# Down-projections of the second MLP as seven products for eight, for 14 of 18 pairs of chunks

## The chip, the cores and the metric

The kernel runs on one core of one Trainium2 chip. The metric is the device time of one execution in microseconds (us), as the median of several runs. The core has TensorE (PE in the rows, with its weight loads as PEld), VectorE (DVE), ScalarE (ACT), GpSimd (POOL, almost unused here) and SyncE (SP), which issues nearly all transfers.

## The reference, cut to what matters

An attention without softmax gives `x` (2304 tokens, 512 features), and two MLPs follow. All is float32; the weights of the MLPs reach the kernel as float64.

```python
h = np.maximum(x @ w_in, 0.0);  x = h * h @ moe_w_out          # first MLP, d_ff 2048
a = x @ w_a;  b = x @ w_b;      out = a * b @ moe2_w_out       # second MLP, d_ff 1536
```

## The kernel before

**Numbers.** A float32 operand of a product is kept as two halves, a rounded one (`[:, 0]`) and the rest (`[:, 1]`). A product of two operands is three matmuls into one PSUM bank: both halves of the weight with the rounded half of the data, and the rounded half of the weight with the rest of the data. ACT makes the rounded half (`copy` into an `F32R` tile), DVE the rest (`sub`). Weights are converted from float64 words to float32 (`w_float`: two ACT and four DVE instructions for 512 columns), kept in DRAM (`keep`), and fetched again for each pass and split in their slot `w` (`fetch`: a transfer, an ACT cast, a DVE subtraction).

**Stages.** After the attention and the first six chunks of the first MLP comes `rest()`: the other ten chunks of the first MLP (ph 1), then the second MLP (ph 2). Both go over the tokens in three passes of 768, each two halves j of N2 = 384 columns. In ph 2 a unit is one chunk c of 128 hidden rows: `group()` computes `a` and `b` of the chunk for both halves of the tokens as seven products for eight (42 matmuls of 384 columns, PSUM banks 4 to 7), with ACT copies from bank to bank and DVE additions between them. What it leaves is `c11` (j = 0) and `c12` (j = 1), which `lower` splits into a tile of the `gh` kind for the down-projection. For each pass `x_prep` makes the seven operands `xo` of the tokens, from seven ACT casts and eleven DVE subtractions of 768 columns, all seven without a second buffer (the seventh lies in `xb`).

**Down-projections.** `out_steps` multiplies a chunk's `gh` tile of one half j with the chunk's 512 down weights: 12 matmuls into banks 0 to 3, one job. Jobs run in runs of up to six chunks for one j and then the other; at a run's end four DVE instructions add the banks to `xt` (`evac`; a pass's first run of each j is copied). A pass has 24 jobs, 288 matmuls, and 20 such evacuations. The jobs trail the units: `due` pays out 12 matmuls' worth for each half of a unit, 2.5 units behind (`LAG`).

**Tiles.** `rest()` has eight float tiles (`ttiles`) for `p5`, `c11`, `c12`, `c22`, eight split tiles (`gtiles`), eight slots `w` for the up weights (four pieces to a unit, fetched two units ahead) and five for down weights. Conversion works in the tiles `wf`, `wl`, `we`, `raw`; the float slots `wf` and `wl` are taken in turn, eight of them.

**Order.** Every instruction is first added to `Plan` with its engines, an estimated duration and its dependencies. `Plan.order` then fixes the order of each engine's queue ahead of time: at each step an engine takes, of the instructions that are ready by the estimates, the one whose latest start is earliest. On the chip each engine follows that fixed order.

Of the kernel before, what the change touches and what calls it, by code (L numbers as in the profile page):

```python
# [22 lines left out]
P = 128  # L23
# [18 lines left out]
PIECES, OUTS = 8, 5  # L42
RUN, LAG = {1: 2, 2: 3}, {1: 4, 2: 5}

# [167 lines left out]
def tile_retention_two_mlps(  # L212
# [36 lines left out]
    def dmac(bytes_):  # L249
        return {"DMA": max(620.0, bytes_ / 260.0)}  # L250

# [61 lines left out]
    raws = []  # L313
    kept = {}

# [101 lines left out]
    def fetch(name, i, n):  # L417

        h, l = ("w", i, 0), ("w", i, 1)
        f = wslot[i].bitcast(F32)  # L420
        plan.add(dmac(P * 4 * n), dma(lambda: f[:, 1, :n], lambda: kept[name]), [("kept", name)], [l])
        plan.add({"ACT": act(n)}, copy(lambda: wslot[i][:, 0, :n], lambda: f[:, 1, :n]), [l], [h])
        plan.add(
            {"DVE": dve(n), "POOL": pool(n)},
            sub(lambda: wslot[i][:, 1, :n], lambda: f[:, 1, :n], lambda: wslot[i][:, 0, :n]), [h], [l],
        )

    def keep_out(name, src):
# [3 lines left out]
    def keep_pair(ph, c, src_a, src_b):  # L432

        a, b = slice(0, 256), slice(256, 512)
        wa, ka = w_float(src_a)
        wb, kb = w_float(src_b)
        keep((ph, c, 0), wa, ka, 512)
        ss, ks, exs = float_slot()

        def op(fn, o, co, x, cx, y, cy, r, w):  # L440
            plan.add(
                {"DVE": dve(256)},
                fn(lambda: o()[:, co], lambda: x()[:, cx], lambda: y()[:, cy]), r, w, exs,
            )
# [7 lines left out]
        keep((ph, c, 3), lambda: wa()[:, b], ka, 256)  # L452

    def keep_first(c):
# [347 lines left out]
    def enter():  # L802
# [39 lines left out]
    def rest():  # L842
# [14 lines left out]
        ttiles += [(lambda i=i: tmp[i][:, :n], ("tmp", i)) for i in range(4)]  # L857
        turn = {"t": 0, "piece": 0}
        gfree = list(gtiles)
        ofree = list(range(PIECES, PIECES + OUTS))  # L860

        def take_t():
            x, k = ttiles[turn["t"] % len(ttiles)]
            turn["t"] += 1
            plan.renew(k)
            return x, k

        def take_g():
            x, k = gfree.pop(0)
            plan.renew(k)  # L870
            return x, k

        def x_prep(ph, p):
# [8 lines left out]

            def parts(o, i, j):
# [13 lines left out]

            parts(0, 0, 0)
            comb((0, 0), (0, 1), (0, 0))
            parts(1, 0, 0)  # L900
            parts(2, 1, 0)
            comb((0, 0), (1, 1), (0, 0))
            parts(3, 0, 0)
            parts(4, 1, 1)
            comb((0, 1), (1, 1), (0, 1))
            parts(5, 0, 1)
            comb((1, 0), (1, 0), (0, 0))
            parts(6, 1, 0)

# [6 lines left out]

        units = [(ph, p, c) for ph in (1, 2) for p in range(PASSES) for c in CHUNKS[ph][::3 - ph]]
        pieces = {}

        def piece(u):  # L920
            for q in range(4):
                i = turn["piece"] % PIECES
                turn["piece"] += 1
                pieces[units[u], q] = i
                fetch((units[u][0], units[u][2], q), i, 256 if q == 3 else 512)

        outs = {}
        wanted = [(ph, p, c) for ph in (1, 2) for p in range(PASSES) for c in CHUNKS[ph]]

        def out_piece():  # L930
            if wanted:
                ph, p, c = wanted.pop(0)
                i = ofree.pop(0)
                outs[ph, p, c] = [i, 2]
                fetch((ph, c, 4), i, 512)


        PRODUCTS = [
            (0, 0, 0, 1, True), (1, 1, 0, 0, True), (3, 2, 0, 2, False), (2, 0, 256, 1, False),
            (5, 2, 256, 3, False), (4, 3, 0, 2, False), (6, 1, 256, 3, False),  # L940
        ]

        def group(unit, banks, fresh):
# [11 lines left out]
            for i, q, s, b, start in PRODUCTS:  # L955
# [14 lines left out]
                elif i == 1:  # L970
                    p5, k5 = take_t()
                    plan.add(pa, copy(p5, lambda: o[0]), [ko[0]], [k5])
                elif i == 2:
                    c11, k11 = take_t()
                    if ph == 2:
# [6 lines left out]
                elif i == 4:  # L982
                    c12, k12 = take_t()
                    plan.add({"DVE": dve(n)}, add(c12, lambda: o[2], p5), [ko[2], k5], [k12])
                    if ph == 2:
                        plan.add({"DVE": dve(n)}, mul(c12, c12, c22), [k22], [k12])
                    else:
                        relu({"ACT": act(n)}, c12, k12, c12, k12)
                        square((ph, p, 1, c), c12, k12)
                elif i == 5:  # L990
                    c22, k22 = take_t()
                    plan.add({"DVE": dve(n)}, add(c22, lambda: o[3], p5), [ko[3], k5], [k22])
# [3 lines left out]
                elif ph == 2:  # L996
                    plan.add({"DVE": dve(n)}, mul(c11, lambda: o[3], c11), [ko[3]], [k11])
                    for j, (g, kg) in enumerate(((c11, k11), (c12, k12))):
                        gh, kgh = take_g()
                        plan.add({"ACT": act(n)}, copy(lambda gh=gh: gh()[:, 0], g), [kg], [kgh + (0,)])  # L1000
                        lower((ph, p, j, c), gh, kgh, g, kg)
                else:
                    c21, k21 = take_t()
                    relu(pa, c21, k21, lambda: o[3], ko[3])
# [5 lines left out]
        def square(name, r, kr):  # L1010
            gh, kgh = take_g()
            plan.add(
# [5 lines left out]
        def lower(name, gh, kgh, g, kg):  # L1018
# [3 lines left out]
            )  # L1022
            made[name] = gh, kgh

        made = {}

        def out_steps(ph, p, j, c, start, last, round_):
            gh, kgh = made.pop((ph, p, j, c))
            c0 = (2 * p + j) * n

            def evac(m):
                d = lambda: xt[:, m, c0:c0 + n]
                kd, a, ka = tokens("xt", m, c0, n), bank[m], ("bank", m)
                if ph == 2 and round_ == 0:
                    plan.add({"ACT": act(n, True), "DVE": dve(n)}, copy(d, lambda: a[:, :n]), [ka], kd)
                else:
                    plan.add({"DVE": dve(n)}, add(d, lambda: a[:, :n], d), [ka], kd)
                if ph == 2 and c == CHUNKS[2][-1]:
                    plan.add(dmac(P * 4 * n), dma(lambda: out[:, m, c0:c0 + n], d), kd)

            wi = outs[ph, p, c][0]
# [11 lines left out]
            for m in range(KT):  # L1053
                if last:
# [3 lines left out]
                    )  # L1058
                    evac(m)
                    yield 3 / 12  # L1060
# [8 lines left out]
            gfree.append((gh, kgh))  # L1069
            outs[ph, p, c][1] -= 1  # L1070
            if not outs[ph, p, c][1]:
                ofree.append(wi)
                out_piece()

        def order(ph):
            cs, at, j, size = CHUNKS[ph], [0, 0], 0, RUN[ph]
            while min(at) < len(cs):
                a, b = at[j], min(at[j] + size, len(cs))
                yield from ((j, cs[i], i == a, i == b - 1, int(a > 0)) for i in range(a, b))
                at[j], j, size = b, 1 - j, 2 * RUN[ph]  # L1080

        downs = (s for ph in (1, 2) for p in range(PASSES) for d in order(ph) for s in out_steps(ph, p, *d))
        due = -LAG[1]

        x_prep(1, 0)
        piece(0)
# [3 lines left out]
        for u, unit in enumerate(units):  # L1090
            ph, p, c = unit
            if u and units[u - 1][:2] != (ph, p):
                x_prep(ph, p)
                if (ph, p) == (2, 0):
                    due -= LAG[2] - LAG[1]
            for _ in group(unit, (4, 5, 6, 7), u == 0):
                due += {1: 4, 2: 2}[ph] / 14
                while due > 1e-6:
                    due -= next(downs)
            if u + 2 < len(units):  # L1100
# [93 lines left out]
```

## Time and profile before

| | us |
|---|---|
| median of 3 runs (862.95 to 863.95) | 863.61 |
| profiled execution, its own time | 864.91 |
| span in its trace, first to last instruction | 863.2 |
| PE busy | 847.3 |
| PEld busy | 816.7 |
| DVE busy | 665.8 |
| ACT busy | 545.8 |

The span lies 1.7 us under the profiled execution's own time. Busy times are of merged intervals: where instructions of one engine overlap, the overlap counts once. A pipelined PE is shown as busy although each matmul's shown duration is longer than the distance to the next.

### The profile page before, as it was taken

How to read it: one execution, taken by the hardware profiler on the slowest of the kernel's cores; microseconds unless marked ns; L12 is line 12 of the kernel's file. 1: busy time of each engine (PE TensorE's matmuls, PEld its weight loads, DVE VectorE, ACT ScalarE, POOL GpSimd, SP SyncE). 2: the span in 40 equal slices, each digit the busy share in tenths (PEclk: the TensorE clock that was granted, in tenths of full speed). 3: DMA queues.
4: the chain of work that ended last, by engine and by line, in shares of the span. 5: the costliest groups of instructions: out<-in, count | busy, mean ns of one | idle time of the engine just before them, and what ended most of it. 6: DMA issues, size and time to landing. Idle time of an engine off the chain costs nothing.

```text
span 863.2 us, 17321 instructions
## 1 busy us (share of the span) xinstructions
PE 847.3 (98%) x6624; PEld 816.7 (95%) x6624; DVE 665.8 (77%) x1338; ACT 545.8 (63%) x1077; POOL 0.7 (0%) x6
## 2 busy tenths in 40 slices
PE   5999999999999999999999999999999999999998
PEld 5888888889999999999999999999999999999998
DVE  5999784987699999999999987597555577655553
ACT  3676562777788787978885665475555465555530
POOL 0000000000000000000000000000000000000000
PEclk9999999999999999999999999999999999999999
DMA  8776872478776678567846876335333344443322
GB/s 298 249 265 216 282 220 60 132 234 259 268 231 194 208 236 245 173 221 249 256 135 214 247 255 213 87 104 171 112 113 110 90 119 129 135 115 93 110 56 74
DMA packets 76195, 154.89 MB, mean 179 GB/s; under 512 B 8400, under 2 KB 20816, under 8 KB 76112
## 3 DMA queue, kind: packets, MB, share of 16 engines
q1 hardware_dynamic: 75968, 153.78, 56.9%
q8 instruction: 52, 0.85, 0.4%
q14 instruction: 31, 0.25, 0.1%
q10 hardware_dynamic: 144, 0.01, 0.0%
HBM read 122.95 MB, written 30.80 MB: 178 GB/s over the span
## 4 chain that ended last, share of the span: by engine, by line
PE 95%; DVE 3%; issue 1%; ACT 0%; DMA 0%; ACTq 0%
PE bank L229 95%; DVE wf L394 1%; DVE wf L383 0%; DMA vt<-vtab 0%; DVE xt L620 0%; DVE sa L657 0%; DVE pt L635 0%; DVE xt L241 0%; DVE wf L375 0%; DVE wf L368 0%; DVE w L238 0%; ACT we L390 0%; ACT tv L548 0%; DVE gh L238 0%; DVE xb L238 0%
## 5 line engine op out<-in xcount | busy, mean ns | idle before, releaser
L229 PE MATMUL bank<-xo,w 128*128 128x384 f32 x1838 | 410.4, 334 | 0.0
L229 PEld LDWEIGHTS bank<-xo,w 128*128 128x128 f32 x1838 | 326.7, 188 | 0.0
L229 PE MATMUL bank<-xb,w 128*128 128x384 f32 (+2 forms) x1050 | 239.7, 347 | 0.9 <-ACT r L759 0.7
L235 ACT CAST w<-w 128x512 fp32r<-128x512 f32 (+1 forms) x270 | 153.4, 579 | 90.0 <-DMA w<-kept 80.4
L229 PEld LDWEIGHTS bank<-xb,w 128*128 128x128 f32 x1050 | 185.8, 188 | 13.4 <-ACT r L759 1.1
L238 DVE TENSOR_TENSOR w<-w 128x512 fp32r<-128x512 f32 (+1 forms) x270 | 169.1, 634 | 24.1 <-ACT w L235 22.4
L229 PE MATMUL bank<-gh,w 128*128 128x384 f32 (+2 forms) x768 | 181.4, 352 | 0.3 <-DVE w L238 0.3
L229 PEld LDWEIGHTS bank<-gh,w 128*128 128x128 f32 x768 | 135.7, 188 | 12.1 <-DVE w L238 0.7
L229 PE MATMUL bank<-w,w 128*128 128x384 f32 x588 | 138.9, 334 | 0.0
L229 PEld LDWEIGHTS bank<-w,w 128*128 128x128 f32 x588 | 105.2, 188 | 0.0
L241 DVE TENSOR_TENSOR xt<-bank,xt 128x384 f32<-128x384 f32 x108 | 59.3, 552 | 18.6 <-PE bank L229 17.6
L235 ACT COPY bank<-bank 128x384 f32<-128x384 f32 x102 | 47.6, 467 | 35.2 <-PE bank L229 34.2
L241 DVE TENSOR_TENSOR tmp<-bank,g 128x384 f32<-128x384 f32 x42 | 23.3, 556 | 48.6 <-PE bank L229 48.5
L229 PE MATMUL bank<-ghl,w 128*128 128x384 f32 x204 | 47.3, 334 | 0.0
L241 DVE TENSOR_TENSOR r<-bank,tmp 128x384 f32<-128x384 f32 x26 | 14.4, 555 | 38.2 <-PE bank L229 38.0
L759 ACT ACTIVATE r<-bank 128x512 f32<-128x512 f32 (+1 forms) x30 | 16.6, 553 | 33.6 <-PE bank L229 33.6
L235 ACT COPY tmp<-bank 128x384 f32<-128x384 f32 (+2 forms) x51 | 24.6, 485 | 20.2 <-PE bank L229 19.5
L229 PEld LDWEIGHTS bank<-ghl,w 128*128 128x128 f32 x204 | 36.4, 188 | 0.0
L238 DVE TENSOR_TENSOR xo<-xt,xo 128x768 fp32r<-128x768 f32 x36 | 33.7, 951 | 3.2 <-ACT xo L235 3.1
L238 DVE TENSOR_TENSOR gh<-g,gh 128x512 fp32r<-128x512 f32 (+2 forms) x41 | 25.1, 611 | 13.1 <-ACT g L762 9.6
L235 ACT CAST xo<-xt 128x768 fp32r<-128x768 f32 x36 | 29.6, 835 | 6.4 <-issue 5.1
L390 ACT ACTIVATE we<-raw 128x512 int32<-128x512 uint32 x48 | 32.1, 669 | 0.3 <-DVE wf L394 0.3
(118 smaller groups left out, 879.8 us busy)
## 6 DMA issues: line engine op xcount, KB each, us to landing
w<-kept SPq DMA_DIRECT2D x219, 256.0 KB, 2.9
raw<-w SPq DMA_DIRECT2D x48, 512.0 KB, 4.4
kept<-wf SPq DMA_DIRECT2D x42, 256.0 KB, 4.1
wraw<-w SPq DMA_DIRECT2D x16, 512.0 KB, 6.6
kept<-wl SPq DMA_DIRECT2D x31, 256.0 KB, 4.0
vr<-vk SPq DMA_DIRECT2D x16, 448.0 KB, 4.7
qkr<-qk SPq DMA_DIRECT2D x16, 448.0 KB, 5.3
w<-kept SPq DMA_DIRECT2D x51, 128.0 KB, 2.4
```

Source lines behind the costliest of these rows:

```text
L229: T.matmul(o, l, r, start=start, stop=stop, skip_group_check=True)
L235: return lambda e: A.copy(o(), i()) if e == "ACT" else eng[e].tensor_copy(o(), i())
L238: return lambda e: eng[e].tensor_sub(o(), a(), b())
L241: return lambda e: eng[e].tensor_add(o(), a(), b())
L390: lambda e: A.activation(like(rest), lo(), AF.Copy, scale=LO_ULPS), [kraw], [ke],
L394: lambda e: V._custom_dve(ADD32_U16LIMBS, out=w().bitcast(U16), in0=w().bitcast(U16), in1=rest.bitcast(U16)),
L759: lambda e, o=o: A.activation(r[:, :n], o[:, :n], AF.Relu), [ko], [kr],
```

## The change

For 14 of the 18 pairs of chunks (2 chunks times 2 halves of the tokens, two blocks of 256 output features) the down-projection is done as seven products for eight too (`sevens`), of 256 output features each, two groups u of 128. A run has three pairs (one has two) and goes product by product: product o for all its pairs into the same banks, with copies from bank to bank and additions to `xt` between products (`side`). The split of the data moves from `lower` into `halve`, seven for a pair of chunks, with four differences (`diff`) before them; until then `c11` and `c12` stay in their float tiles, and 14 more are lent from the conversion's tiles at unit 6 of pass 0 (`MORE`). The weights of the seven products, sums and differences of the down weights, are made once, after conversion (`keep_outs`), and fetched as halves of a slot (`half_slot`, 256 columns). A run starts when its last chunk's unit is done, and is paid out over 0.8 of its number of units (`SPAN`) by `target`, which takes the place of `due`; `LAG` is now counted in units. Piece 0 of each chunk's up weights is stored split after its first use and fetched split in the later passes (`PARTS`). The estimate for transfers goes from 260 to 310 bytes per ns.

```diff
-RUN, LAG = {1: 2, 2: 3}, {1: 4, 2: 5}
+RUN, LAG = {1: 2, 2: 3}, {1: 1, 2: 2.5}
+SEVENS = {(2, 0): [range(6, 12)], (2, 1): [range(0, 6), range(6, 12)], (2, 2): [range(0, 6), range(6, 10)]}
+AFTER = 0.0
+SPAN = 0.8
+MORE = (2, 0, 6)
+PARTS = (0,)
...
-        return {"DMA": max(620.0, bytes_ / 260.0)}
+        return {"DMA": max(620.0, bytes_ / 310.0)}
...
+    def half_slot(i, s):
+
+        flat = wslot[i].rearrange("p h n -> p (h n)")
+        return flat[:, 512 * s:512 * s + 512].rearrange("p (h n) -> p h n", h=2)
...
+    def fetch_to(name, cols, to, h, l, n):
+
+        hl = [h] if h == l else [h, l]
+        for start, stop in ((cols.start, cols.stop), (0, 512)):
+            if (name, start, stop) in parts:
+                p, cs = parts[name, start, stop], slice(cols.start - start, cols.stop - start)
+                plan.add(
+                    dmac(P * 8 * n), dma(lambda: to().bitcast(F32), lambda: p[:, :, cs]),
+                    [("parts", name, start, stop)], hl,
+                )
+                return
...
+        if name[0] == 2 and name[2] in PARTS and later(name):
+            p = dram.tile([P, 2, n], F32, name="parts" + "_".join(map(str, (*name, cols.start))))
+            parts[name, cols.start, cols.stop] = p
+            plan.add(
+                dmac(P * 8 * n), dma(lambda: p, lambda: to().bitcast(F32)), hl,
+                [("parts", name, cols.start, cols.stop)],
+            )
...
+    def keep_outs(c):
+
+        a, b = slice(0, 256), slice(256, 512)
+        wa, ka = w_float(w2[c, :, 2, :])
+        wb, kb = w_float(w2[c + 1, :, 2, :])
+        keep((2, c, 4), wa, ka, 512)
+        keep((2, c + 1, 4), wb, kb, 512)
+        (s, ks, exs), (t, kt, ext) = float_slot(), float_slot()
...
+        op(add, s, a, wa, b, wb, b, [ka, kb], [ks], exs)
+        op(sub, s, b, s, a, wa, a, [ka], [ks], exs)
+        op(sub, t, a, wa, a, wa, b, [ka], [kt], ext)
+        op(sub, t, b, wb, a, s, b, [kb, ks], [kt], ext)
+        keep((2, c, 5), s, ks, 512)
+        keep((2, c, 6), t, kt, 512)
...
-        for c in CHUNKS[2]:
-            keep_pair(2, c, w2[c, :, 0, :], w2[c, :, 1, :])
-            keep_out((2, c, 4), w2[c, :, 2, :])
+        for c in CHUNKS[2][::2]:
+            for d in (c, c + 1):
+                keep_pair(2, d, w2[d, :, 0, :], w2[d, :, 1, :])
+            keep_outs(c)
...
+        more = [(lambda i=i: rings["wf"][0][i][:, :n], ("wf", i)) for i in range(WF)]
+        more += [(lambda i=i: floats[i][:, :n], ("wf", WF + i)) for i in range(WL)]
+        more += [(lambda i=i: rings["we"][0][i].bitcast(F32)[:, :n], ("we", i)) for i in range(WE)]
+        more += [
+            (lambda i=i, j=j: raws[i].bitcast(F32)[:, 512 * j:512 * j + n], ("late", i))
+            for i in range(RAWS) for j in range(2)
+        ]
...
+                    if run:
+                        k = at[ph, p, run[-1]] + 1 if ph == 2 else at[ph, p, run[-2]] + 1
+                        jobs.append(("sevens", ph, p, run, len(run) * 21 / 12, k + AFTER, None, cs[0] == CHUNKS[ph][0]))
+                        cs = cs[len(run):]
+                        continue
...
+                    fresh = part[0] == CHUNKS[ph][0]
+                    k0 = at[ph, p, part[0] - (part[0] - CHUNKS[1][0]) % 2 if ph == 1 else part[0]] + LAG[ph]
+                    k1 = k0 + len(part) / (2 if ph == 1 else 1)
...
+            if job[0] == "sevens":
+                jobs[x] = job[:6] + (min(nxt, job[5] + SPAN * len(job[3]) / (2 if job[1] == 1 else 1)),) + job[7:]
...
+        def target(v):
+            t = 0.0
+            for job in jobs:
+                a, b = job[5], job[6]
+                t += job[4] * min(1.0, max(0.0, (v - a) / (b - a)))
+            return t
...
+        ORDER = [(0, 4, 0, 0), (1, 4, 0, 0), (0, 5, 0, 0), (0, 5, 1, 0), (0, 6, 0, 0), (0, 6, 1, 0), (1, 4, 1, 0)]
...
+                        if unit in sevened:
+                            made[ph, p, j, c] = g, kg
+                            continue
...
+        def put(ph, p, m, j, b, fresh, done):
+
+            c0 = (2 * p + j) * n
+            d = lambda: xt[:, m, c0:c0 + n]
+            kd, a, ka = tokens("xt", m, c0, n), bank[b], ("bank", b)
+            if ph == 2 and fresh:
+                plan.add({"ACT": act(n, True), "DVE": dve(n)}, copy(d, lambda: a[:, :n]), [ka], kd)
+            else:
+                plan.add({"DVE": dve(n)}, add(d, lambda: a[:, :n], d), [ka], kd)
...
+        def sevens(x, ph, p, run, fresh, done):
+
+            cs = run[::2]
+            raw = {
+                (c, i, j): made.pop((ph, p, j, c + i)) for c in cs for i in range(2) for j in range(2)
+            }
+
+            def diff(c, o, a, b):
+                (to, kt), (u, ku), (v, kv) = raw[c, *o], raw[c, *a], raw[c, *b]
+                plan.add({"DVE": dve(n)}, sub(to, u, v), [ku, kv], [kt])
+
+            def halve(c, o):
+                (g, kg), (gh, kgh) = raw[c, *o], take(gfree)
+                plan.add({"ACT": act(n)}, copy(lambda: gh()[:, 0], g), [kg], [kgh + (0,)])
+                plan.add(
+                    {"DVE": dve(n)}, sub(lambda: gh()[:, 1], g, lambda: gh()[:, 0]), [kg, kgh + (0,)], [kgh + (1,)]
+                )
+                return gh, kgh
+
+            def drop(c, o):
+                tfree.append(raw.pop((c, *o)))
+
+            def prepare(o):
+                got = []
+                for c in cs:
+                    b11, b12, b21, b22 = (0, 0), (0, 1), (1, 0), (1, 1)
+                    if o == 0:
+                        got.append(halve(c, b11))
+                        diff(c, b11, b12, b11)
+                    elif o == 1:
+                        got.append(halve(c, b21))
+                    elif o == 2:
+                        got.append(halve(c, b11))
+                        diff(c, b11, b22, b11)
+                        diff(c, b12, b22, b12)
+                    elif o == 3:
+                        got.append(halve(c, b11))
+                        diff(c, b21, b21, b11)
+                        drop(c, b11)
+                    else:
+                        x = (b12, b22, b21)[o - 4]
+                        got.append(halve(c, x))
+                        drop(c, x)
+                return got
+
+            def side(o, u):
+                b, a = u, 2 + u
+                kb, ka = ("bank", b), ("bank", a)
+                pa = {"ACT": act(n, True)}
+                if o == 0:
+                    plan.add(pa, copy(lambda: bank[a][:, :n], lambda: bank[b][:, :n]), [kb], [ka])
+                elif o == 1:
+                    put(ph, p, u, 0, b, fresh, done)
+                elif o == 2:
+                    put(ph, p, u, 1, b, fresh, False)
+                    put(ph, p, 2 + u, 1, b, fresh, False)
+                elif o == 3:
+                    plan.add(pa, copy(lambda: bank[b][:, :n], lambda: bank[a][:, :n]), [ka], [kb])
+                elif o == 4:
+                    put(ph, p, 2 + u, 1, b, False, done)
+                elif o == 5:
+                    put(ph, p, u, 1, a, False, done)
+                else:
+                    put(ph, p, 2 + u, 0, b, fresh, done)
+
+            got = prepare(0)
+            for o in range(7):
+                now, got = got, prepare(o + 1) if o < 6 else []
+                for u in range(2):
+                    b = u + 2 if o in (3, 5) else u
+                    for c, (gh, kgh) in zip(cs, now):
+                        i, t = outs[x, o, c]
+
+                        def f(e, o=o, u=u, b=b, c=c, gh=gh, i=i, t=t):
+                            w, cols, a = half_slot(i, t), slice(u * P, u * P + P), bank[b][:, :n]
+                            first = o in (0, 2) and c == cs[0]
+                            mm(a, w[:, 0, cols], gh()[:, 0], first, False)
+                            mm(a, w[:, 1, cols], gh()[:, 0], False, False)
+                            mm(a, w[:, 0, cols], gh()[:, 1], False, c == cs[-1])
+
+                        plan.add(mmc(n, n, n), f, [("w", i, t), kgh + (0,), kgh + (1,)], [("bank", b)])
+                        yield 3 / 12
+                    side(o, u)
+                for c, g in zip(cs, now):
+                    gfree.append(g)
+                    used(outs[x, o, c][0])
...
+            if unit == MORE:
+                tfree.extend(more)
+            for k, _ in enumerate(group(unit, (4, 5, 6, 7), u == 0)):
+                goal = target(u + (k + 1) / 14)
+                while due < goal - 1e-6:
+                    due += next(downs)
```

## Rows read from the trace of the kernel before

**Rows 1.** The page: span, then busy us, share of the span, instructions.

```profile
span 863.2 us, 17321 instructions
...
PE 847.3 (98%) x6624; PEld 816.7 (95%) x6624; DVE 665.8 (77%) x1338; ACT 545.8 (63%) x1077; POOL 0.7 (0%) x6
```

**Rows 2.** The chain that ended last: start, us, what; its last pieces.

```profile
70.02 788.06 PE bank L229 x5470
858.11 2.12 DVE xt L241 x4
```

**Rows 3.** Windows: stretch, us, busy time of each engine, PEclk, DMA share, GB/s.

```profile
0.00:70.00 70.00, 57.65 (x1145) 49.47 (x1145) 56.78 (x152) 42.21 (x79) 0.67 (x6) 0.95 0.79 275
263.00:446.00 183.00, 183.00 (x1057) 182.88 (x1056) 176.34 (x335) 154.83 (x311) 0.00 (x0) 1.00 0.70 220
446.00:528.00 82.00, 82.00 (x475) 82.00 (x474) 76.27 (x157) 54.06 (x109) 0.00 (x0) 1.00 0.71 227
497.00:530.00 33.00, 33.00 (x192) 33.00 (x192) 29.29 (x61) 21.52 (x44) 0.00 (x0) 1.00 0.77 248
528.00:537.00 9.00, 9.00 (x54) 9.00 (x53) 5.69 (x12) 5.16 (x11) 0.00 (x0) 1.00 0.70 200
583.00:720.00 137.00, 137.00 (x792) 137.00 (x792) 87.06 (x158) 73.39 (x145) 0.00 (x0) 1.00 0.40 115
```

**Rows 4.** Timeline of DVE: start us, us, instruction, count.

```profile
438.71 0.95 DVE L238 TENSOR_TENSOR xt<-xt 128x768 f32<-128x768 f32 x1
439.58 0.95 DVE L238 TENSOR_TENSOR xo<-xt,xo 128x768 fp32r<-128x768 f32 x1
...
449.52 0.68 DVE L238 TENSOR_TENSOR w<-w 128x512 fp32r<-128x512 f32 x1
450.12 0.55 DVE L241 TENSOR_TENSOR xt<-bank,xt 128x384 f32<-128x384 f32 x1
450.59 0.54 DVE L244 TENSOR_TENSOR tmp<-tmp,tmp 128x384 f32<-128x384 f32 x1
...
451.52 0.41 DVE L238 TENSOR_TENSOR w<-w 128x256 fp32r<-128x256 f32 x1
451.86 0.55 DVE L238 TENSOR_TENSOR xb<-tmp,xb 128x384 fp32r<-128x384 f32 x1
...
465.20 0.42 DVE L368 TENSOR_SCALAR wf<-wf 128x512 f32<-128x512 f32 x1
465.53 0.55 DVE L241 TENSOR_TENSOR xt<-bank,xt 128x384 f32<-128x384 f32 x1
```

**Rows 5.** Groups by form: count, busy us, mean ns, idle before.

```profile
L235 ACT CAST w<-w 128x512 fp32r<-128x512 f32 x219 | 134.2, 620 | 88.3 <-DMA w<-kept 79.1 <-PE bank L229 8.7
L235 ACT COPY bank<-bank 128x384 f32<-128x384 f32 x102 | 47.6, 467 | 35.2 <-PE bank L229 34.2
L241 DVE TENSOR_TENSOR tmp<-bank,g 128x384 f32<-128x384 f32 x42 | 23.3, 556 | 48.6 <-PE bank L229 48.5
L235 ACT CAST w<-w 128x256 fp32r<-128x256 f32 x51 | 20.6, 403 | 1.6 <-DMA w<-kept 1.3 <-PE bank L229 0.3
L235 ACT CAST w<-tmp 128x384 fp32r<-128x384 f32 x15 | 7.6, 514 | 2.3 <-DVE tmp L244 1.8
```

**Rows 6.** Transfers: tiles, queue, count, KB each, median us to landing.

```profile
w<-kept SPq DMA_DIRECT2D x219, 256.0 KB, 2.9
kept<-wf SPq DMA_DIRECT2D x42, 256.0 KB, 4.1
w<-kept SPq DMA_DIRECT2D x51, 128.0 KB, 2.4
```

**Rows 7.** Timeline of DVE: pair operations, last conversion, c22 of units 7 and 8.

```profile
503.25 0.41 DVE L238 TENSOR_TENSOR wf<-wl,wf 128x256 f32<-128x256 f32 x1
...
525.11 0.42 DVE L238 TENSOR_TENSOR wf<-wf,wl 128x256 f32<-128x256 f32 x1
...
525.78 0.55 DVE L241 TENSOR_TENSOR r<-bank,tmp 128x384 f32<-128x384 f32 x1
...
527.06 0.69 DVE L394 CUSTOM_DVE_ANT_0 wl<-wl,we 128x1024 uint16<-128x1024 uint16 x1
...
536.92 0.56 DVE L241 TENSOR_TENSOR tmp<-bank,g 128x384 f32<-128x384 f32 x1 [1.49 <-PE bank L229]
```

**Rows 8.** Windows of L383, one instruction to a conversion: stretch, us, DVE busy (count).

```profile
497.00:530.00 33.00, 3.41 (x5) 1.00 0.77 248
```

**Rows 9.** Timeline of DVE: first and last operand of one x_prep, of seven.

```profile
565.90 0.96 DVE L238 TENSOR_TENSOR xo<-xt,xo 128x768 fp32r<-128x768 f32 x1 [0.20 <-ACT xo L235]
...
579.57 0.95 DVE L238 TENSOR_TENSOR xb<-xt,xb 128x768 fp32r<-128x768 f32 x1
```

More of the change, by code (lines that the diff above doesn't have):

```diff
@@ L313, in tile_retention_two_mlps @@
     raws = []
-    kept = {}
+    kept, parts = {}, {}
     def raw_slot():
@@ L917, in rest @@
         units = [(ph, p, c) for ph in (1, 2) for p in range(PASSES) for c in CHUNKS[ph][::3 - ph]]
+        at = {unit: u for u, unit in enumerate(units)}
         pieces = {}
         def piece(u):
+            pass_["now"] = units[u][1]
             for q in range(4):
@@ new lines, in rest @@
+        final = {}
+        for x, job in enumerate(jobs):
+            final[job[1], job[2]] = x
+        for x, job in enumerate(jobs):
+            nxt = jobs[x + 1][5] if x + 1 < len(jobs) else job[5] + 99
+            if job[0] == "sevens":
+                jobs[x] = job[:6] + (min(nxt, job[5] + SPAN * len(job[3]) / (2 if job[1] == 1 else 1)),) + job[7:]
+            elif job[6] > nxt:
+                jobs[x] = job[:6] + (nxt,) + job[7:]
+        def target(v):
[4 more added lines that the diff above has]
+            return t
@@ new lines, in rest @@
+        ORDER = [(0, 4, 0, 0), (1, 4, 0, 0), (0, 5, 0, 0), (0, 5, 1, 0), (0, 6, 0, 0), (0, 6, 1, 0), (1, 4, 1, 0)]
+        outs = {}
+        wanted = []
+        for x, job in enumerate(jobs):
+            kind, ph, p, what = job[:4]
+            if kind == "plain":
+                for c in dict.fromkeys(r[1] for r in what):
+                    wanted.append((p, [("whole", (ph, p, c), (ph, c, 4))]))
+            else:
+                todo = []
+                for o, (d, e, s, _) in enumerate(ORDER):
+                    for c in what[::2]:
+                        todo.append(("half", (x, o, c), (ph, c + d, e), s))
+                wanted += [(p, todo[i:i + 2]) for i in range(0, len(todo), 2)]
@@ new lines, in rest @@
+        uses = {}
+        def out_piece():
+            if not wanted:
+                return
+            p, todo = wanted.pop(0)
+            pass_["now"] = p
+            i = ofree.pop(0)
+            plan.renew(("w", i))
+            uses[i] = 2 if todo[0][0] == "whole" else len(todo)
+            for t, what in enumerate(todo):
+                outs[what[1]] = i, t
+                if what[0] == "whole":
+                    fetch(what[2], i, 512)
+                else:
+                    fetch_half(what[2], what[3], i, t)
@@ L938, in rest, with used @@
+        def used(i):
+            uses[i] -= 1
+            if not uses[i]:
+                ofree.append(i)
+                out_piece()
         PRODUCTS = [
@@ L941, in rest @@
         ]
+        sevened = {(job[1], job[2], c) for job in jobs if job[0] == "sevens" for c in job[3]}
         def group(unit, banks, fresh):
@@ L1010, in square @@
         def square(name, r, kr):
-            gh, kgh = take_g()
+            if name[0:2] + name[3:] in sevened:
+                plan.add({"ACT": act(n)}, lambda e: A.activation(r(), r(), AF.Square), [], [kr])
+                made[name] = r, kr
+                return
+            gh, kgh = take(gfree)
             plan.add(
@@ L1023, in lower, with plain @@
             made[name] = gh, kgh
+            tfree.append((g, kg))
         made = {}
-        def out_steps(ph, p, j, c, start, last, round_):
-            gh, kgh = made.pop((ph, p, j, c))
[L1029 to L1039, printed above, removed]
+        def put(ph, p, m, j, b, fresh, done):
[6 more added lines that the diff above has]
+                plan.add({"DVE": dve(n)}, add(d, lambda: a[:, :n], d), [ka], kd)
+            if done:
+                plan.add(dmac(P * 4 * n), dma(lambda: out[:, m, c0:c0 + n], d), kd)
+        def plain(ph, p, j, c, start, last, fresh, done):
+            gh, kgh = made.pop((ph, p, j, c))
             wi = outs[ph, p, c][0]
@@ L1069, in out_steps @@
             gfree.append((gh, kgh))
[L1070 to L1080, printed above, removed]
@@ new lines, in lowers @@
+        def lowers():
+            for x, job in enumerate(jobs):
+                kind, ph, p, what = job[:4]
+                end = ph == 2 and final[ph, p] == x
+                if kind == "plain":
+                    for j, c, start, last, fresh in what:
+                        tail = end and last and c == what[-1][1]
+                        yield from plain(ph, p, j, c, start, last, fresh, tail)
+                else:
+                    yield from sevens(x, ph, p, what, job[7], end)
+        downs = lowers()
@@ L1085, in rest @@
+        due = 0.0
         x_prep(1, 0)
```

105 lines of the change are left out of this document (62 added, 43 removed).

## The prediction

> **What bounds the kernel now.** I read the page first: PE is busy for 98% of the span, DVE 77%, ACT 63% [rows 1]. Busy time of a pipelined PE proves little, so the chain of waits comes next: from 70.02 us to the last matmul it is one piece of 788.06 us on PE, and only four DVE additions and the output's transfers stand behind it [rows 2]. The second MLP is bound by the number of its matmuls. The windows give their price: one pass, 792 matmuls, takes 137.0 us [rows 3], 0.173 us each. In that pass DVE has 87.06 us of work, ACT 73.39. Before it, where the down-conversion of weights runs, DVE is nearly full: 176.34 of 183 us from 263 to 446 [rows 3]. Noise: below 0.2%, 1.7 us, two runs of this kernel can't be told apart.
>
> DVE and ACT instructions overlap a little, so I price them by distance from start to start [rows 4]: 0.335 us for 256 columns (and for 512 of a conversion's instructions with one tensor), 0.467 for 384, 0.602 for 512, 0.868 for 768.
>
> **PE.** A pair of chunks had 4 jobs of 12 matmuls, 48; it now has 7 products of 2 groups u, 3 matmuls each: 42. 14 pairs save 84, 84 x 0.173 = 14.53 us. A pass saves 18, 36 and 30 matmuls: 3.1, 6.2 and 5.2 us. The Trainium skill, "TensorE: Matmul & The Clock Gate", section "Back-to-back issue gap", gives N / 2.4 + 2.5 ns for a matmul that stands alone, 162.5 ns at 384 columns; by it the sum would be 13.65 us. The trace differs: 173 ns, with the weight load busy all the time beside it [rows 3]; the measurement decides.
>
> **DVE and ACT in a pass.** What is hidden has to fit beside 756 matmuls, 130.8 us, in pass 1, where all pairs are changed. DVE before, by count and price: up weights 12 x (3 x 0.602 + 0.335) = 25.7; down weights 12 x 0.602 = 7.2; 48 instructions on the units 22.4; `lower` 24 x 0.467 = 11.2; 12 additions to `xt` 5.6 (8 of 20 are copies, mostly on ACT); `x_prep` 11 x 0.868 = 9.5; together 81.6 (merged busy time 87.06). After: up weights lose one split of 512 in each unit, 18.5; down weights 42 x 0.335 = 14.1; units 22.4; `diff` 24 x 0.467 = 11.2; `halve` 42 x 0.467 = 19.6; 16 additions 7.5; `x_prep` 9.5; together 102.8, which the same ratio makes 109.7 of 130.8, 84%. DVE has been fuller than that without PE waiting [rows 3]. ACT loses 24 casts of 512 columns and gets 42 of 256, 18 of 384 and 8 copies more: -14.9 + 16.9 + 9.3 + 3.7 = 15.0 [rows 5], 88 of 130.8 us, 68%. So on average nothing but PE sets the pace, and these edits cost nothing; if DVE could use only 80% of its time, the pass would last 137 us and its gain would be gone.
>
> **Transfers.** A down fetch becomes two of 128 KB, which land in 2.4 us against 2.9 for 256 KB [rows 6]; piece 0 of 512 KB replaces 256 KB, two units ahead. A pass moves some 6 MB more, from 115 to about 160 GB/s, where 220 were reached without PE waiting [rows 3]. On SP's queue a pass has 90 fetches for 60. I cost this at nothing. The other estimate for transfers can reorder every queue, the first 70 us too, where PE idles for 12.35 us [rows 3]; no row shows which way, and I bound it by 0.8 us of gain, a fifteenth of that idle time, and as much of loss.
>
> **Three waits that it may bring.**
>
> First, the lent tiles. Float tiles are handed out in turn: units 6 and 7 use the eight old ones, and unit 8 of pass 0 takes `wf` 0 to 3. `p5` of unit 8, an ACT copy out of bank 4, needs `wf` 0. Of the 75 float slots taken by the conversion (15 for the first MLP, 10 for each of 6 pairs) number 72 counted from 0 is the last on `wf` 0: the down weights of chunk 11, nearly the last of all. So the copy waits for the end of conversion and for the store. In the kernel before, the last conversion ends at 527.75 us; a store lands 4.1 us later [rows 6, 7]; with 0.48 for the copy `p5` would be there at 532.3, and `c22` of unit 8, which reads it, starts at 536.92 [rows 7]. That leaves 4.6 us. `keep_outs` adds 24 DVE instructions of 256 columns, 8.0 us; units 6 and 7 lose four `lower`, 1.9; net 6.1. DVE idles for 9.0 us between 446 and 537 [rows 3]. If it can use that, the wait is nothing; if conversion goes ahead of all else, 6.1 - 4.6 = 1.5; if it gets only its present share, it is later: five conversions [rows 8] of 1.88 (2 x 0.335 + 2 x 0.602) and eight pair operations [rows 7] fill 12.1 of the 33 us up to 530, with 3.7 of idle time [rows 3] 48%, so 6.1 / 0.48 = 12.7 late, and the wait 8.1. `Plan.order` knows the due time and pulls conversion forward, so I take 1.0, between the first two. Behind `p5` stand the next copies on ACT, `c22`, and product 6 on PE; what PE has left then is about one job of 2 us.
>
> Second, `x_prep` at the two pass ends. Its seven operands took 565.90 to 580.5, 14.6 us [rows 9], within units of 11.4. The unit before a boundary will now have no down-projections: 42 x 0.173 = 7.27 us, 1.04 a product, and the run that starts in the next unit gives that one 68 matmuls, 1.69 a product. From the first operand free (1.04) to the seventh needed (7.27 + 6 x 1.69 = 17.4) there are 16.4 us, 1.8 more than it took. The first `halve` and `diff` of the new run want 4.2 us of DVE there. If all of that goes in front, 2.4 us are lost; if none, nothing. I take 0.3, twice.
>
> Third, units without down-projections. Downs pause for units 1 to 2.5 of pass 0, 8.5 to 12, and for 1.2 units at the end of each of the next three runs: 8.6 units. In the trace `c22` comes 11.1 us after the one before it [rows 7]; a pure unit has 7.27, and no row shows one. In each, three hand-overs (two copies between banks, `c22`) must fall within one product's 1.04 us. The loop through one bank, copy, product, copy, product, addition, is 0.467 + 1.04 + 0.467 + 1.04 + 0.556 = 3.6 us [rows 5] and hand-overs, under 7.27, and the next unit's first two products can go in front; so a throughput bound is excluded, but an order fixed by estimates isn't exact. If each of 26 hand-overs waits for half a cast, 0.31 us [rows 5], that is 8.0 us; below, nothing. Near the lower end because of the loop's slack: 1.0.
>
> The end stays as it is: the last two chunks are plain, and four additions and the transfers follow as now [rows 2].
>
> **Sum.** 863.61 - 14.53 + 1.0 + 0.6 + 1.0 = 851.7 us. The trace is of an execution of 864.91 us with a span of 863.2; the same sum puts the new span at 851.3.
>
> **Rivals.**
>
> A, the forecast: PE stays the bound. 848.4 (no wait, and 0.8 from the start) to 854. For it: no wait of PE in 788 us while DVE was 96% busy in a stage. 70%.
>
> B, the lent tiles bind: conversion has only its present share, the wait is 8.1 in place of 1.0: 858.8; the case takes in 854 to 861.9. For it: DVE is full there, and ACT waits long for fetches [rows 5]. Against: DVE's 9 us of idle time, and a due time that the order knows. 15%.
>
> C, slower: pure units are bound by the hand-overs between PE, ACT and DVE. If each of the 26 waits for a whole cast and its own copy, 0.62 + 0.47 = 1.09, 28 us are lost: 849.1 + 28 = 877. It is slower than before by more than 0.2% from 14.5 + 1.7 = 16.2 us, 0.62 a hand-over, a unit of 9.2 us for 7.27. For it: no such unit is in the trace, and four banks are all that a unit has. Against: the loop above. The Trainium skill, "Perfetto Trace Analysis", section "Optimization Strategy", reads the same gap coming back on the engine that should be full as a sign of too little SBUF or PSUM for the next tile; no run here shows such gaps yet. 9%.
>
> D, the same: DVE at 84% of a pass with products in fixed order can use only 80%, and passes 1 and 2 gain nothing: 863.61 - 3.1 + 2.6 = 863.1. Against: 96% in another stage. 6%.
>
> **How the numbers follow.** The likeliest is A, 851.7. Faster by over 0.2%: A and B, 85%; within: D, 6%; slower: C, 9%. The range leaves out C, D and the part of B above 859.0, with a trifle below 848.4: 848.4 to 859.0.
>
> **What the next profile would show.** 6540 matmuls for 6624, still 0.173 us apart. The chain one piece on PE from about 70 us; gaps, if any, at unit 8 of pass 0 behind an ACT copy into `wf`, at the pass ends behind `xo`, or one for each pure unit behind copies between banks. DVE about 84% busy in pass 1, down additions not the releaser of PE. Wrong it would be by a gap of several us at unit 8, by gaps that return with each run, or by a first stage that is longer or shorter than 70 us.

## The result, and the profile after

The changed kernel takes 853.7 us (median of 4 runs, 851.67 to 854.88) against 863.31 for the kernel before, a ratio of 0.9885 with a 95% interval of 0.9865 to 0.9906. It is faster, 2.0 us above the forecast of 851.7 and inside its range. Its four runs lie 3.2 us apart, those of the kernel before 1.0.

The page of the kernel after, to be read beside [rows 1]: span, then busy us, share of the span and instructions of each engine.

```profile
span 852.4 us, 17685 instructions
...
PE 834.8 (98%) x6540; PEld 801.4 (94%) x6540; DVE 731.9 (86%) x1531; ACT 565.9 (66%) x1180; POOL 0.7 (0%) x6
```

The 84 matmuls are gone, DVE has 66 us more. Windows of the kernel after, in the columns of [rows 3]: about one pass each.

```profile
575.00:706.00 131.00, 131.00 (x755) 130.48 (x755) 106.67 (x216) 80.90 (x184) 0.00 (x0) 1.00 0.53 163
706.00:837.00 131.00, 130.91 (x755) 130.59 (x754) 109.91 (x234) 77.97 (x185) 0.00 (x0) 1.00 0.48 144
```

DVE is busy for 106.67 and 109.91 of 131 us, where 109.7 of 130.8 was worked out for a pass with all its pairs changed; ACT for 80.90 and 77.97, where 88 was; transfers run at 163 and 144 GB/s, where 160 was. So the loads were near, ACT's 7 to 10 us too high. The chain of the kernel after is no longer one piece as in [rows 2]. Its pieces from 430 to 545 us: start, us, what.

```profile
433.61 14.32 PE bank L234 x81
...
451.57 5.09 DMA raw<-w
456.66 0.02 issue
456.68 0.68 ACT wf L369
457.36 0.39 ACT bank L240
457.75 0.04 issue
457.79 34.38 PE bank L234 x196
492.17 3.61 DMA w<-kept
...
522.29 8.12 PE bank L234 x46
530.41 4.14 DMA w<-kept
```

Read from the top: PE's piece of 34.38 us begins when a copy between banks on ACT is done; that copy stood behind an instruction of the conversion on the same queue, and this one waited for a transfer of raw words. The same place in ACT's timeline, and one 300 us later; what stands in brackets is the idle time before the instruction and what ended it.

```profile
455.31 0.51 ACT L240 CAST xb<-r 128x384 fp32r<-128x384 f32 x1 [1.15 <-DVE r L249]
456.68 0.68 ACT L369 ACTIVATE wf<-raw 128x512 f32<-128x512 f32 x1 [0.85 <-DMA raw<-w]
457.25 0.48 ACT L240 COPY bank<-bank 128x384 f32<-128x384 f32 x1
...
621.75 0.62 ACT L240 CAST w<-w 128x512 fp32r<-128x512 f32 x1 [2.62 <-DMA w<-kept]
622.27 0.47 ACT L240 COPY bank<-bank 128x384 f32<-128x384 f32 x1
```

ACT was idle, with an instruction at the head of its queue whose transfer had not landed, and the copy that PE needed was next. The transfers land later than before [rows 6]: median us in the last column, over the whole kernel.

```profile
w<-kept SPq DMA_DIRECT2D x167, 256.0 KB, 3.7
...
w<-kept SPq DMA_DIRECT2D x149, 128.0 KB, 3.0
w<-parts SPq DMA_DIRECT2D x24, 512.0 KB, 3.5
```

Part of that rise is the mix of stages: the changed kernel fetches fewer pieces of 256 KB in its passes, and a second profile of it has 3.4 in the first row. In like stretches, 575 to 706 us, 256 KB land in 2.7 us before and in 3.2 after, in both profiles.

**Where the time went.** PE shows as busy in short waits, so I took the distances from start to start of neighbouring 384-column matmuls and added up what each is above 173.3 ns. The first of them starts at 211 us; what lies before is in the first row. From the two traces, in us:

```
                                       before    after   difference
first matmul of 384 columns starts     211.73   211.13        -0.60
84 matmuls fewer, 0.1733 each                               -14.56
sum above 173.3 ns                       0.26     3.91        +3.65
last matmul starts                     859.30   847.80       -11.50
from there to the span's end             3.88     4.57        +0.69
```

The gain in matmuls is the forecast one; 3.65 us of it are given back in some ten short waits, the longest 0.67 us at 457 us. The trace lists eight of them as waits of the weight loads: six, 2.4 us, for a copy between banks on ACT, and two, 1.0 us, for an addition on DVE.

### The profile page after: what moved, and what is told of

The parts are those of the page before. It is cut to its first block, busy times and chain, and to the rows that moved or that the text cites. A ratio compares the mean times of both kernels' runs of the same rounds, so it can differ in the third digit from the quotient of the medians.

```text
span 852.4 us, 17685 instructions
## 1 busy us (share of the span) xinstructions
PE 834.8 (98%) x6540; PEld 801.4 (94%) x6540; DVE 731.9 (86%) x1531; ACT 565.9 (66%) x1180; POOL 0.7 (0%) x6
## 4 chain that ended last, share of the span: by engine, by line
PE 86%; DMA 6%; DVE 4%; ACT 3%; issue 1%; SPq 0%; ACTq 0%; DVEq 0%
PE bank L234 86%; DMA w<-kept 2%; DMA raw<-w 2%; DMA wraw<-w 1%; ACT w L240 1%; DMA vr<-vk 1%; DVE w L243 1%; DVE xt L246 1%; DMA vt<-vtab 0%; DVE wf L388 0%; ACT tv L613 0%; ACT xb L240 0%; DVE wf L399 0%; ACT wf L369 0%; ACT bank L240 0%
## 5 line engine op out<-in xcount | busy, mean ns | idle before, releaser
L234 PE MATMUL bank<-xo,w 128*128 128x384 f32 x1838 | 389.5, 335 | 0.9 <-ACT bank L240 0.7
L234 PE MATMUL bank<-xb,w 128*128 128x384 f32 (+2 forms) x1044 | 229.1, 347 | 1.1 <-ACT r L824 0.8
L234 PE MATMUL bank<-gh,w 128*128 128x384 f32 (+2 forms) x750 | 171.9, 352 | 0.2
L234 PE MATMUL bank<-w,w 128*128 128x384 f32 x546 | 123.9, 334 | 0.1
L234 PEld LDWEIGHTS bank<-w,w 128*128 128x128 f32 x546 | 97.1, 188 | 0.5 <-DVE xt L246 0.4
L246 DVE TENSOR_TENSOR xt<-bank,xt 128x384 f32<-128x384 f32 x128 | 69.7, 552 | 8.4 <-PE bank L234 7.9
L240 ACT COPY bank<-bank 128x384 f32<-128x384 f32 x122 | 57.2, 469 | 16.5 <-PE bank L234 13.9
L399 DVE CUSTOM_DVE_ANT_0 wf<-wf,we 128x1024 uint16<-128x1024 uint16 x45 | 30.7, 685 | 0.4
L613 ACT ACTIVATE tv<-vr,vt 128x448 f32<-128x448 f32 (+1 forms) x32 | 15.0, 500 | 21.5 <-DMA vr<-vk 19.7
L234 PE MATMUL bank<-tv,vr 64*64 64x64 f32 x512 | 20.5, 233 | 8.6 <-ACT tv L613 8.6
```

The source lines that it names most:

```text
L234: T.matmul(o, l, r, start=start, stop=stop, skip_group_check=True)
L240: return lambda e: A.copy(o(), i()) if e == "ACT" else eng[e].tensor_copy(o(), i())
L246: return lambda e: eng[e].tensor_add(o(), a(), b())
L399: lambda e: V._custom_dve(ADD32_U16LIMBS, out=w().bitcast(U16), in0=w().bitcast(U16), in1=rest.bitcast(U16)),
L613: lambda e, to=to, ti=ti, q=q: A.activation(self.tv[:, to], self.v[:, ti], AF.Copy, scale=vt[:, NP + q:NP + q + 1]),
```

## The experiments

Twelve kernels were run, in three lots on three chips, each lot with the kernel before beside it (863.34, 863.3 and 863.68 us). The ratio is to that kernel, with its 95% interval; the sum of gaps is the one above, from one profiled execution of each.

```
                                     us       ratio   interval            gaps
the change again                  854.03     0.9891   0.9875 to 0.9907    5.25
estimate 260                      855.25     0.9915   0.9900 to 0.9929    7.94
before with 310                   866.08     1.0037   1.0023 to 1.0050    1.67
landing 3.0                       850.33     0.9851   0.9837 to 0.9864    0.19
all pairs plain, landing 3.0      864.80     1.0023   1.0010 to 1.0036    0.27
estimate 260, float slots last    849.57     0.9843   0.9830 to 0.9857    1.41
15 pairs, landing 3.0             848.93     0.9846   0.9824 to 0.9867    0.16
no split pieces                   851.83     0.9872   0.9857 to 0.9887    2.49
float slots last                  854.14     0.9891   0.9878 to 0.9905    4.65
15 pairs, 3.0, float slots last   848.61     0.9828   0.9814 to 0.9841    0.47
before with landing 3.0           863.80     1.0002   0.9993 to 1.0011    0.14
15 pairs, 3.0, slots last, 260    853.36     0.9877   0.9864 to 0.9891    5.44
```

**The change again**, as a control.

> The changed kernel itself, once more, as the control for the others on this chip. Theory (late fetches): on ACT's fixed queue the cast of a fetched weight stands ahead of a copy between banks, and where the transfer lands later than the order supposed, both wait and PE behind them; such waits vary from execution to execution, so the times spread over some 3 us again, 851.5 to 855. Rival (units without down-projections bound by hand-overs, or the lent tiles): these waits are of fixed length, the spread would be under 1 us around 853.7.

854.03 us, 851.78 to 855.55: the spread of the first four runs came back, 3.8 us for 3.2; four runs prove little by their spread. The gaps of its profile are 5.25 us, partly at other times than in the first profile.

**The estimate for transfers back at 260.**

```diff
-        return {"DMA": max(620.0, bytes_ / 310.0)}
+        return {"DMA": max(620.0, bytes_ / 260.0)}
```

> Only the estimate for transfers goes back from 310 to 260 bytes per ns; all else as changed. Late fetches, with the lower estimate as their cause: the casts move back in ACT's queue, gaps of PE in the second MLP fall from 3.7 to about 1.5 us, and the time is 851 to 852. Rival, the waits come from the added traffic or from hand-overs and not from the estimate: 853 to 854.5, gaps of 3 to 4 us as before.

855.25 us: neither theory. Up to 450 us the gaps are gone, and 7.2 us of new ones lie between 500 and 600. The chain of this kernel there:

```profile
544.27 5.78 DMA kept<-wl
550.05 0.02 issue
550.07 0.57 DVE wl L246
...
550.72 0.47 ACT bank L240
551.19 0.04 issue
551.23 4.97 PE bank L234 x18
```

PE waits for a copy, the copy for an addition of unit 9 into a lent float slot (`wl`), the addition for the store of converted weights out of that slot, which landed 5.78 us after its issue. This is the wait on lent tiles that the prediction had placed one unit earlier. DVE's timeline shows why it is here and not in the changed kernel: the last instruction of `keep_outs`, first in the changed kernel, then in this one.

```profile
526.29 0.42 DVE L243 TENSOR_TENSOR wl<-wl,wl 128x256 f32<-128x256 f32 x1
```

```profile
541.98 0.42 DVE L243 TENSOR_TENSOR wl<-wl,wl 128x256 f32<-128x256 f32 x1
```

**The kernel before with the estimate of 310 alone.**

```diff
-        return {"DMA": max(620.0, bytes_ / 260.0)}
+        return {"DMA": max(620.0, bytes_ / 310.0)}
```

> The kernel before with only the estimate changed, 310 for 260 bytes per ns. Late fetches by the estimate: waits of PE appear in a kernel that had none, 864 to 866. Rival, the estimate alone does nothing without the added traffic: 863.3, within 0.5 us, no gap of PE over 0.1 us after the start.

866.08 us, 2.7 slower, as the theory of late fetches expects (864 to 866). The gaps of its profile, 1.67 us, lie between 250 and 420 us, where conversion runs, none behind it. The profiled execution took 865.54 us, the shortest of its five runs, and that of the kernel before 864.91, so the two traces don't hold the whole 2.7 us; where the rest lies I did not find.

**The landing supposed as 3.0 us.** The order takes a transfer's result as ready 3.0 us after its estimated end, not 2.1.

```diff
-    LAT = {"PE": 200, "DMA": 2100, "ACT": 160, "DVE": 150}
+    LAT = {"PE": 200, "DMA": 3000, "ACT": 160, "DVE": 150}
```

> The changed kernel, with the time from a transfer's end to its use supposed as 3.0 us in the order for 2.1; nothing but the order of the queues changes. Late fetches: the order now supposes landings about as late as the trace shows them (3.0 to 3.7 us), casts stand behind the copies that come first, gaps fall under 1.5 us, 850 to 851.5. Rival (hand-overs or lent tiles): unchanged, 853 to 854.5, since neither depends on transfers.

850.33 us, and the spread falls to 1.5. The sum of gaps is 0.19. The chain of this kernel is one piece again:

```profile
69.24 773.44 PE bank L234 x5386
842.70 2.12 DVE xt L246 x4
```

The transfers are no faster than in the control, whose page has 3.4 us for 256 KB as well. The rows of this run:

```profile
w<-kept SPq DMA_DIRECT2D x167, 256.0 KB, 3.4
...
w<-kept SPq DMA_DIRECT2D x149, 128.0 KB, 2.9
```

What changed is who waits for them. The waits of ACT from 440 to 850 us (total us, times, longest), first of the changed kernel, then of this one:

```profile
ACT w L240 <- DMA w<-kept: 52.2, 45, 4.3
```

```profile
ACT w L240 <- DMA w<-kept: 10.2, 14, 2.3
```

And the same place in ACT's timeline as above, where the first copy of that unit now stands ahead of the conversion's next instruction:

```profile
454.28 0.52 ACT L240 CAST xb<-r 128x384 fp32r<-128x384 f32 x1 [1.07 <-DVE r L249]
455.25 0.46 ACT L240 COPY bank<-bank 128x384 f32<-128x384 f32 x1 [0.45 <-PE bank L234]
...
460.90 0.68 ACT L369 ACTIVATE wf<-raw 128x512 f32<-128x512 f32 x1 [1.02 <-DMA raw<-w]
```

The units without down-projections are in this kernel too. DVE's timeline, `c22` and `c12` of units 8 and 9:

```profile
535.33 0.56 DVE L246 TENSOR_TENSOR wf<-bank,wf 128x384 f32<-128x384 f32 x1 [0.33 <-PE bank L234]
536.37 0.56 DVE L246 TENSOR_TENSOR wf<-bank,wf 128x384 f32<-128x384 f32 x1 [0.15 <-PE bank L234]
543.13 0.56 DVE L246 TENSOR_TENSOR wl<-bank,wl 128x384 f32<-128x384 f32 x1 [0.35 <-PE bank L234]
```

A unit in 7.80 us (three matmuls of a down-projection are among its 45), products 1.04 us apart, and no gap of PE: four banks and their hand-overs are enough. The constant reorders every engine's queue, so that it is ACT's queue that counts is read from these rows and was not tried alone.

**All pairs plain, with 3.0 us.**

```diff
-SEVENS = {(2, 0): [range(6, 12)], (2, 1): [range(0, 6), range(6, 12)], (2, 2): [range(0, 6), range(6, 10)]}
+SEVENS = {}
```

> The landing time supposed as 3.0 us as in the run that did so, and no pair of chunks as seven products: all 18 pairs plain, with everything else of the change kept (sums and differences of the down weights made and stored but not used, split pieces, lent tiles, the schedule of the jobs). If the gain is the 84 matmuls and nothing else, this is 14.5 us above the same kernel with 14 pairs: 864.9, with no gap of PE. Rival, the surroundings of the change (split pieces, lent tiles, other lags) carry part of it: 862 or less.

864.80 us, 14.47 above the same kernel with 14 pairs (the two ran in different lots; the kernel before agrees in them to 0.04 us). Its eleven runs reach from 863.70 to 869.97. The gain is the matmuls, and the rest of the change gives nothing by itself; it costs 1.5 us against the kernel before, and no trace shows where.

**Estimate 260, float slots last.** The order in which the lent tiles are handed out:

```diff
-        return {"DMA": max(620.0, bytes_ / 310.0)}
+        return {"DMA": max(620.0, bytes_ / 260.0)}
...
-                tfree.extend(more)
+                tfree.extend(more[8:] + more[:8])
```

> The estimate back at 260 bytes per ns, where PE waited 7.7 us in its profile, most of it from 539 to 560 us, and the lent tiles handed out in another turn: the tiles of words first, the float slots last, so that units 9 and 10 no longer write float slots whose stores to DRAM are still under way. Lent tiles as the cause of that wait: the gaps from 539 to 560 fall under 1.5 us, and the time from 855.25 to 850 to 851.5. Rival, the wait comes from late fetches there too and the store named beside it is chance: 854 to 856.

849.57 us, 5.7 below 260 alone; gaps of 1.41 for 7.94, and 1.1 from 500 to 600 us for 7.2. The wait at 260 was that of the lent tiles.

**Float slots last, with the change's own estimates.**

```diff
-                tfree.extend(more)
+                tfree.extend(more[8:] + more[:8])
```

> The changed kernel with its own estimates (310 bytes per ns, 2.1 us to use) and only the turn of the lent tiles changed, float slots last. Late fetches alone hold the changed kernel back: no effect, 853 to 854.5, gaps of 3 to 5 us in the same places. Rival, the lent tiles hold it back as they did at 260: 850 to 851.5.

854.14 us, no effect on the time, gaps of 4.65. They are not in the same places: 3.2 us of them lie before 446 us (0.9 in the changed kernel, 2.1 in the control) and 1.4 behind it (3.0 and 3.1). That the lent tiles cost the changed kernel nothing rests on its chain too: from 205 us on it has no store out of a lent slot, in either of its two profiles.

Against the run above this one differs by the estimate alone, 310 for 260, and takes 4.6 us longer (two lots; 4.1 by the ratios). 3.2 us of that are gaps. So with the lent tiles out of the way the estimate of 310 is by itself a cause of the waits.

**Without the split pieces.**

```diff
-PARTS = (0,)
+PARTS = ()
```

> The changed kernel with its own estimates, without the split pieces: piece 0 is fetched as 256 KB and split anew in each pass, as in the kernel before; 15 MB less traffic, 24 more casts on ACT and 24 more subtractions on DVE. Late fetches by added traffic: landings get shorter, gaps fall, 852 to 853. Late fetches by the supposed landing time alone: more casts behind transfers on ACT's queue, so as many gaps or more, 854 to 857.

851.83 us, below both ranges and 2.2 under the control, with gaps of 2.49. The rows of its transfers:

```profile
w<-kept SPq DMA_DIRECT2D x191, 256.0 KB, 2.9
...
w<-kept SPq DMA_DIRECT2D x149, 128.0 KB, 2.5
```

256 KB land in 2.9 us, as before the change [rows 6]. By the medians 24 casts and subtractions more cost less than the traffic that they replace; the four runs, 850.80 to 853.57, overlap the control's, so this is likely and not shown.

**The kernel before with 3.0 us.**

```diff
-    LAT = {"PE": 200, "DMA": 2100, "ACT": 160, "DVE": 150}
+    LAT = {"PE": 200, "DMA": 3000, "ACT": 160, "DVE": 150}
```

> The kernel before with the landing time supposed as 3.0 us and nothing else. Late fetches: it had no gap of PE to lose, so 862.8 to 863.8, the same. Rival, the gain of the supposed landing time in the changed kernel lies elsewhere (the first 70 us, the end) and would show here too: 859 to 861.

863.80 us, the same. It had no such wait to lose, which fits the 3.7 us that the supposed landing gives the changed kernel being its waits.

**15 pairs, with 3.0 us.**

```diff
-SEVENS = {(2, 0): [range(6, 12)], (2, 1): [range(0, 6), range(6, 12)], (2, 2): [range(0, 6), range(6, 10)]}
+SEVENS = {(2, 0): [range(6, 12)], (2, 1): [range(0, 6), range(6, 12)], (2, 2): [range(0, 6), range(6, 12)]}
...
-    LAT = {"PE": 200, "DMA": 2100, "ACT": 160, "DVE": 150}
+    LAT = {"PE": 200, "DMA": 3000, "ACT": 160, "DVE": 150}
```

> The landing time supposed as 3.0 us and the last pair too as seven products, 15 of 18, so that the last run has three pairs and ends the pass. Only the number of matmuls counts: 6 fewer, 1.0 us less, 849.3. Rival, the tail pays for it: the last run can start its first product only when the last unit is through, its 126 matmuls have no up-projections beside them, so PE waits for halves and differences made by ACT and DVE, and the four additions become more: 851 to 855.

848.93 us, three runs at 848.5 to 849.2 and one at 853.41; 1.4 under 14 pairs in the medians, 1.0 by the count. The gaps, 0.16, show no price in the tail.

**15 pairs, 3.0 us, float slots last**: the last two edits with the turn of the lent tiles.

> 15 pairs, the landing time supposed as 3.0 us and the float slots lent last. By both mechanisms nothing is left to wait for: 848.5 to 849.3, no gap of PE over 0.2 us after 70 us. If the turn of the lent tiles matters only where the order puts conversion late, it is the same as 15 pairs without it, 848.9.

848.61 us, 848.34 to 849.84, ratio 0.9828 (0.9814 to 0.9841). This is the best version found, ahead of both kernels; it can't be told from 15 pairs without the turn.

**The same with the estimate at 260.**

> As the 15 pairs with 3.0 us and the float slots lent last, with the estimate back at 260 bytes per ns. If both the estimates only have to be late enough, the same, 848.5 to 849.3; if the first stage gains from 260, as the run with 260 and the other turn of the lent tiles began its first matmul of 384 columns 1.7 us earlier, 847 to 848.

853.36 us, a miss. DVE's timeline in it, the last instruction of `keep_outs`:

```profile
550.31 0.42 DVE L243 TENSOR_TENSOR wl<-wl,wl 128x256 f32<-128x256 f32 x1 [0.90 <-DMA kept<-wl]
```

Conversion ends at 550.7 us (522.7 in the best version), and the gaps, 5.44 us, lie at 535 to 572, where PE waits for additions on DVE into lent slots. The chain from 534.8 to 545.9 us is DVE's own work, without a store in it, so the first of these waits are for a full DVE and not for a lent slot. With two late suppositions about transfers the order puts conversion too late; that it is the order's single queue for transfers that does it was only argued.

## Why the prediction was right, and where its steps failed

**PE, 14.53 us.** Right: 14.56 by the trace's count, 14.47 by the run with all pairs plain. The 13.65 that the prediction set beside it doesn't fit the 173.3 ns of either trace; the runs alone could not tell the two apart.

**DVE and ACT.** Right in cost, and in size but for ACT, which was put 7 to 10 us too high: DVE is busy for 81 to 84% of a pass, and at that load (106.14 of 131 us from 575 to 706) the run with 3.0 us shows no wait of PE. The rival in which DVE could use only 80% is refuted.

**The lent tiles, 1.0 us.** 0 in the changed kernel (float slots last: no effect). The kind of chain was right and shown at 260, where it cost 5.7 us, though in unit 9 and behind an addition, not in unit 8 behind `p5`. In the changed kernel conversion ended at 526.7 us for 527.75 before [rows 7], with 24 instructions more; at 260, ordered by the same rule, it ended at 542.4. So rival B was a real one, one constant away.

**`x_prep`, 0.6, and units without down-projections, 1.0.** Both 0: the run with 3.0 us has these stretches and no gaps. Rival C, the only one on the slower side, is refuted.

**Transfers, costed at nothing: the step that failed.** DVE's load and the GB/s were near what was worked out, but I compared only throughput, and priced no wait for a landing. The order supposed transfers there sooner than they were, and on ACT's fixed queue the instructions that wait for them stand ahead of the copies that PE needs. It cost some 3.7 us (854.03 to 850.33 by the supposed landing alone), more than the three waits that I had priced (2.6). Longer landings alone don't make the waits: the run with 260 and the float slots last has the changed kernel's 3.2 us for 256 KB from 575 to 706 us, and gaps of 1.41 us in all. [Rows 5] held the sign: ACT idled for 79.1 us before its casts, and I read it only as a point for rival B. It was harmless there. From 440 to 850 us ACT waited longer for fetches in the kernel before than in the changed one (52.2 us, the longest 4.3), and PE had hardly a gap:

```profile
ACT w L235 <- DMA w<-kept: 73.6, 69, 2.4
```

So the sum of ACT's waits is not the price; what stands behind them is. I take it that in longer units a copy could be late without PE noticing, which was argued and not tried alone.

**The estimate of 310, bounded by 0.8 us either way.** Too narrow: alone it costs the kernel before 2.7 us. In the changed kernel going back to 260 costs 1.2, because it uncovers the lent tiles; with these out of the way it gains over 4 us. With the landing at 3.0 it is the other way round, and 260 costs 4.7 (853.36 against 848.61): the two constants act together, and the supposed landing alone removes all gaps. The split pieces may add some 2 us. The lower bound was mis-added too: 849.1 less 0.8 is 848.3, not 848.4.

**Luck in the number.** The 2.6 us priced for three waits came to nothing. They stood in for 3.7 us of waits that I had put at nothing and for the 1.5 us that the rest of the change costs. The matmuls' gain was foreseen; that the time came out only 2.0 us above the forecast is in part luck.

## What to carry to other kernels

An operation that waits for a transfer must not stand ahead of one that the bound engine needs on an in-order queue; when the queues are written out ahead of time, the supposed landing must be that of the loaded kernel: raising one constant by 0.9 us gave back 3.7 us here. A change that adds traffic is checked for landing times, not only for GB/s. And a second mechanism can lie just under the first: judge a correction by the places of the gaps, not by the total time.

## What the runs showed of the hardware that I had not expected

Landings lengthened well below the highest rate. From 575 to 706 us, 256 KB landed in 2.7 us (median) at 116 GB/s in the kernel before, in 2.6 at 138 without the split pieces, and in 3.2 at 163 in the changed kernel; the first 70 us of the kernel before ran at 275 [rows 3]. The rate alone doesn't set it: from 263 to 446 us in the kernel before, at 220 GB/s, they took 3.3. What in the traffic does was not tried alone.

Times spread by 3.2, 3.8 and 2.4 us between four executions where the order of the queues leaned on landings (the changed kernel, again, and with the float slots last), and by 1.5 with the landing at 3.0. But 15 pairs with 3.0, a run with gaps of 0.16 us, spread by 4.9, so the spread settles nothing.
